# A planned RWKV-6 and feed-forward kernel: the planner's buffer rule, one chunk's banks, the fill products and the step order are changed

## The chip, the cores and the metric

The kernel runs on one core of a Trainium2 chip. A core has five engines, each with its own queue of instructions, worked in order: TensorE (PE) multiplies matrices into PSUM, VectorE (DVE) and ScalarE (ACT) do elementwise work, GpSimd (POOL) too, and SyncE (SP) issues transfers. The metric is the device time of one execution in microseconds (us), the median of several runs: before the change 566.9 us over 5 runs, from 564.67 to 569.37.

## The reference

First comes an RWKV-6 attention over 4 sequences, 8 heads, 768 tokens and 48 channels. Its output, 3072 tokens of 384 values, goes through a feed-forward layer of 2048 hidden values with a hard-swish. The weights of that layer come as float64, the rest as float32.

```python
state = np.zeros((B, H, D, D), dtype=np.float32)
for t in range(S):
    cur = np.einsum('bhd,bhe->bhde', u[None] * kt, vt)
    y[:, :, t] = np.einsum('bhd,bhde->bhe', rt, state + cur)
    state = wt[:, :, :, None] * state + np.einsum('bhd,bhe->bhde', kt, vt)
...
h = x @ w_in
relu6 = np.clip(h + 3.0, 0.0, 6.0)
g = h * relu6 / 6.0
return (g @ w_out).astype(np.float32)
```

## The kernel before

**Tiling.** The tokens are cut into 24 chunks of 128 (number i), and four chunks make a block (0 to 5). A chunk's attention is done for all heads at once, in two halves of 64 tokens. A block's 512 tokens then go through the feed-forward layer. Block 0 uses plain products, since its weights are still being loaded and converted from float64; blocks 1 to 5 use sums of weights and of operands, so that fewer products are needed. The feed-forward work of block b runs while the attention of block b+1 is made.

**Steps.** No instruction is written in its final place. Each piece of work is a named step, added to a planner (class Plan) with its engine, an assumed duration, the steps it comes after, a due time (key) and the buffers it holds until named steps have ended. Plan.order walks through an assumed time: of the engine that is free first it takes the open step with the lowest key that can start then. The instructions are emitted in that order, engine by engine, and the chip's queues keep it: a step that waits holds up all steps behind it on its engine.

The names that matter here, with i a chunk and b a block:

- SP: feat, tok, rkt (a chunk's inputs), fetch (weights), refetch (inputs read again for the vets), move, store.
- DVE: back and fore (scans of the decay), own (products for the diagonal), above (line 482, copies the masked scores out of two PSUM buffers, which gives them back), mid and state (the state), shift, join, full (float64 weights to float32), gate (hard-swish), sin and sout (sums of weights), tx (sums of operands), sum (sums of g), reads such as a3 or a10 (line 805), c12 and c22 (results), vet (checks the input range).
- ACT: diag (A's diagonal), turned (K out of PSUM), kvs, third and leave (y out of PSUM into x), low and whole (float64 weights), ramp and clip (hard-swish), s1, c11, c21.
- PE: dot, score, turn, kv; first and read (y of a chunk in block 0); begin and read (y of a later chunk; read also makes the next chunk's scores, in two buffers); up and down (feed-forward). up0.f.c is f of 16 products on chunks from c; upb.d.r is one of 20 products of half d; downb.p.k.x is part x of product k of pair p.
- POOL, from chunk 7 on: K, R, own, decay, decb.

**PSUM.** The tile "bank" is a ring of four PSUM buffers shared by score, up and down; "bankS" is one buffer; "y_ps" is a pair of banks for a chunk's y (and the next chunk's K-times-V in its free columns). The planner holds a count for each ring: a step that needs a buffer may start when enough of the held ones have ended, whichever these are. When the instructions are emitted, the tile pool gives out the real buffers by its own rule.

**Fill products.** Until the first up product, the emitter puts products without use (spin, line 1204) in front of PE steps that the plan starts late, one for each 0.22 us of three quarters of the gap. They write to "bank" buffers. One product of 512 columns (line 296) writes "bankS" at the start.

## Time and profile before

| what | value |
|---|---|
| runs, median (range) | 566.9 us (564.67 to 569.37) |
| profiled execution, its own time | 567.81 us |
| its span | 565.7 us |
| granted TensorE clock, mean | 0.99 |
| PE, DVE, ACT, POOL busy | 543.9, 453.1, 266.4, 105.2 us |
| moved by DMA | 63.96 MB, mean 113 GB/s |
| first up product starts | 31.81 us |
| first product of block 1, 2, 3, 4 starts | 151.25, 237.91, 323.44, 409.69 us |

The page gives each engine's busy time and its share of the span, then the span in 40 slices of 14 us with a digit for the busy tenths, and a row PEclk with the granted clock. A timeline row reads: start, duration, engine, line, operation, tile written and tiles read, shapes, number of records; in brackets, how long the engine was idle before it and what ended that. A product is two records. "Start to start" is the time from one step's first record to the next step's, which is what a step costs PE when nothing waits; a record's own duration is longer, since products overlap. PE's steps cost, start to start: up0 1.30 us, later up products 0.86, down products 1.30 (1.39 in block 0), read 1.52, begin 1.04. DVE's: join and full 0.88 and 0.87, gate 0.33 (block 0) and 0.60, sum of g 0.60, tx 1.71, 1.13, 0.79, 0.79, vet 1.66 for wflat or two times 0.86.

### The profile page before, as it was taken

What the parts mean: (1) busy time and instruction counts of PE and PEld (TensorE: products, weight loads), DVE (VectorE), ACT (ScalarE), POOL (GpSimd) and SP (SyncE); (2) the same over time, 40 slices, a digit from 0 to 9 for tenths busy, and PEclk for the clock granted to TensorE, in tenths of its full rate; (3) what the DMA queues carried; (4) which work ended last, traced back from release to release, by engine and by line L of the source; (5) the groups of instructions that cost most, each with busy time, mean ns of one, the idle gap of its engine ahead of it and who ended that gap; (6) DMA issues with size and microseconds to landing.
All of it is one profiled execution on the core that took longest, in us unless ns stands there. A gap on an engine that the chain in (4) does not pass through costs nothing.

```text
span 565.7 us, 13312 instructions
## 1 busy us (share of the span) xinstructions
PE 543.9 (96%) x5530; PEld 483.2 (85%) x5530; DVE 453.1 (80%) x727; ACT 266.4 (47%) x655; POOL 105.2 (19%) x111
## 2 busy tenths in 40 slices
PE   8999999999999999999998999998999999999995
PEld 7887787678887899888998988898988899988995
DVE  6989999999988977889997889997887836187440
ACT  3876784543365613556613555623465621255100
POOL 2000000126163114211334310425210100000000
PEclk9979999989999999999999999999999999999999
DMA  8949652631240365547423548333400001000001
GB/s 269 290 133 320 216 174 67 169 99 42 87 120 1 89 212 144 175 164 215 127 86 120 173 138 238 92 126 120 142 36 0 9 2 36 30 0 2 0 15 48
DMA packets 23077, 63.96 MB, mean 113 GB/s; under 512 B 3120, under 2 KB 10352, under 8 KB 23008
## 3 DMA queue, kind: packets, MB, share of 16 engines
q1 hardware_dynamic: 22880, 63.02, 35.9%
q8 instruction: 45, 0.74, 0.6%
q14 instruction: 24, 0.20, 0.1%
q10 hardware_dynamic: 128, 0.00, 0.0%
HBM read 57.31 MB, written 4.72 MB: 110 GB/s over the span
## 4 chain that ended last, share of the span: by engine, by line
PE 67%; DVE 24%; issue 3%; DMA 3%; ACT 2%; SPq 0%; DVEq 0%
PE bank L845 26%; PE bank L788 19%; PE bankS L845 5%; PE bank L674 4%; PE bankS L788 3%; DVE g L805 3%; DVE g L813 2%; PE y_ps L549 2%; DMA feat_in<-in_feat_dram 1%; DVE E L407 1%; DVE A L482 1%; PE ps L491 1%; PE y_ps L558 1%; DVE W L416 1%; DVE w_out L394 1%
## 5 line engine op out<-in xcount | busy, mean ns | idle before, releaser
L809 ACT ACTIVATE clip<-g,three 128x512 f32<-128x512 f32 x80 | 57.2, 720 | 55.9 <-DVE g L805 49.9
L805 DVE TENSOR_TENSOR g<-bank,g 128x512 f32<-128x512 f32 x80 | 54.2, 685 | 15.8 <-PE bank L788 15.3
L813 DVE SCALAR_TENSOR_TENSOR g<-clip,g 128x512 f32<-128x512 f32 x80 | 58.2, 737 | 10.7 <-ACT clip L809 10.7
L845 PE MATMUL bank<-w_out,g 128*128 128x192 f32 x352 | 62.6, 328 | 0.0
L845 PEld LDWEIGHTS bank<-w_out,g 128*128 128x128 f32 x352 | 57.9, 190 | 0.8
L427 POOL TENSOR_TENSOR K<-feat_in,E 112x512 f32<-112x512 f32 x17 | 22.1, 1299 | 150.1 <-DVE W L416 93.4
L466 ACT ACTIVATE A<-eyes,dg 128x64 f32<-128x64 f32 x192 | 48.9, 335 | 1.0 <-PE y_ps L558 0.5
L674 PE MATMUL bank<-xT,w_in 128*128 128x256 f32 x192 | 46.2, 393 | 0.0
L674 PEld LDWEIGHTS bank<-xT,w_in 128*128 128x128 f32 x192 | 36.9, 197 | 6.5 <-DVE A L482 0.5
L788 PE MATMUL bank<-xT,w_in 128*128 128x256 f32 x160 | 41.1, 381 | 1.1 <-DVE g L805 1.0
L641 ACT COPY xT<-y_ps 48x256 f32<-48x256 f32 x80 | 29.2, 365 | 25.8 <-PE y_ps L558 25.0
L861 ACT ACTIVATE o<-bank 128x192 f32<-128x192 f32 x33 | 10.9, 332 | 64.1 <-PE bank L845 64.1
L803 ACT COPY g<-bank 128x512 f32<-128x512 f32 x50 | 29.0, 580 | 19.6 <-PE bank L788 19.3
L788 PEld LDWEIGHTS bank<-xT,w_in 128*128 128x128 f32 x160 | 29.9, 190 | 5.6 <-DVE g L805 1.9
L431 POOL TENSOR_TENSOR W<-feat_in,W 112x512 f32<-112x512 f32 x17 | 21.7, 1274 | 62.9 <-DVE W L416 62.9
L407 DVE TENSOR_TENSOR_SCAN E<-feat_in,back 112x520 f32<-112x520 f32 x24 | 30.9, 1288 | 2.8 <-POOL K L427 1.6
L845 PE MATMUL bank<-more,g 128*128 128x192 f32 x176 | 30.7, 327 | 0.6 <-DVE o L863 0.6
L845 PE MATMUL bankS<-w_out,g 128*128 128x192 f32 x176 | 30.5, 327 | 0.8 <-ACT bankS L854 0.8
L788 PE MATMUL bank<-xT,bits 128*128 128x256 f32 x120 | 30.8, 379 | 0.0
L416 DVE TENSOR_TENSOR_SCAN W<-feat_in,start 112x520 f32<-112x520 f32 x24 | 29.5, 1230 | 0.3
L845 PEld LDWEIGHTS bankS<-w_out,g 128*128 128x128 f32 x176 | 28.8, 190 | 1.1 <-ACT bankS L854 1.1
L845 PEld LDWEIGHTS bank<-more,g 128*128 128x128 f32 x176 | 28.7, 190 | 1.0 <-DVE o L863 0.9
(278 smaller groups left out, 1163.0 us busy)
## 6 DMA issues: line engine op xcount, KB each, us to landing
feat_in<-in_feat_dram SPq DMA_DIRECT2D x23, 675.9 KB, 5.5
bits<-in_moe_w_in_dram SPq DMA_DIRECT2D x8, 768.0 KB, 9.6
bits<-in_moe_w_out_dram SPq DMA_DIRECT2D x8, 768.0 KB, 5.3
feat_in<-in_moe_w_in_dram SPq DMA_DIRECT2D x8, 768.0 KB, 4.6
feat_in<-in_moe_w_out_dram SPq DMA_DIRECT2D x8, 768.0 KB, 4.8
rk_in<-in_tok_dram SPq DMA_DIRECT2D x15, 384.0 KB, 5.6
v_in<-in_tok_dram SPq DMA_DIRECT2D x24, 192.0 KB, 3.7
out_dram<-o SPq DMA_DIRECT2D x24, 192.0 KB, 2.0
```

Of the source, the lines that this page charges most:

```text
L407: nc.vector.tensor_tensor_scan(out=E_[:, ::-1], data0=d["w"][:, :0:-1], data1=back.rearrange("q p t -> q (p t)")[:, ::-1], initial=0.0, op ...
L416: nc.vector.tensor_tensor_scan(out=W_, data0=d["w"][:, :-1], data1=starts[i % 2].rearrange("q p t -> q (p t)"), initial=0.0, op0=ALU.mult, ...
L427: early(i).tensor_mul(d["K"], d["k"], d["E"][:, :, 1:])
L466: nc.scalar.activation(out=d["A"][:, h, :], in_=eyes, func=ACT.Copy, scale=d["dg"][:, h])
L641: nc.scalar.copy(out=blocks[bk]["xT"][g * GP:g * GP + D, :, at:at + HL], in_=st[i]["y_ps"][(g ^ a) * GP:(g ^ a) * GP + D, a, :, :])
L674: nc.tensor.matmul(h_ps[:, :(c1 - c0) * L], lhsT=w_in[:, f // 2, j, f % 2, :], rhs=b["xT"][:, j, c0 * L:c1 * L], start=(j == 0), stop=(j = ...
L788: nc.tensor.matmul(b["p", d, c][:, z * HB:(z + 1) * HB], lhsT=weight(W_PLACE[r])[:, 2 * z + d, :], rhs=x_at(bk, X_PLACE[r]), start=fresh a ...
L803: nc.scalar.copy(out=out_, in_=src)
L805: nc.vector.tensor_tensor(out=out_, in0=src, in1=out_of(bk, d, other), op=ALU.add if sign > 0 else ALU.subtract)
L809: nc.scalar.activation(out=c, in_=out_of(bk, d, u), func=ACT.Relu, bias=three, scale=1.0)
L813: nc.vector.scalar_tensor_tensor(out=g, in0=blocks[bk]["r", d, u], scalar=6.0, in1=g, op0=ALU.min, op1=ALU.mult)
L845: nc.tensor.matmul(b["d", p, to][:, :h], lhsT=a, rhs=w(), start=(f == 0 and k in (1, 5)), stop=(f == HF - 1 and k in (2, 3, 4)), skip_grou ...
```

## The change

Five things change.

- The planner keeps a list of the buffers of each ring with the steps that free them. A step takes, of those whose freeing steps are already placed, the buffer whose last freeing step was placed first, and waits for that one buffer.
- Chunk 1's y no longer lies in "y_ps" but in two buffers of "bank"; third1 is four copies instead of two.
- The fill products write to a quarter of "bankS" in turn, only the first with start set; four of them stand at the start, in place of the 512-wide product. The emitter counts 0.28 us for one, and puts none before the first up product. There are 27 in the gaps instead of 39.
- Assumed durations and transfer sizes: those of first, third, read and leave of block 0 are larger, and those of the transfers change (a feature load counts 735 KB instead of 690, a fetch 546 instead of 768).
- The constants that set due times (LAG to TX) are new, and with them the order of steps on every engine. All steps and all instructions other than those above stay the same.

```diff
-LAG = 8.196
-AHEAD = -4.96
-LEAD = -2.25
+LAG = 11.816
+AHEAD = -12.641
+LEAD = 3.239
...
-START = (-127.21, -154.12, -36.12, -115.85, 30.64, 32.42)
-CONV = (-75.91, 4.42)
...
+APART = 1
+START = (-122.25, -133.43, -35.45, -193.52, 38.16, -10.0)
+CONV = (-81.21, 7.03)
...
-    SPIN = 0.22
+    SPIN = 0.28
...
+    def slot(self, r, slots, at, taken):
+
+        open_ = [(max((at[a] for a in frees or ()), default=-1), n) for n, frees in enumerate(slots[r])
+                 if (r, n) not in taken and all(a in at for a in frees or ())]
+        return min(open_)[1] if open_ else None
...
-                for n_, (r, _) in enumerate(hold):
-                    over = len(held[r]) + [x[0] for x in hold[:n_]].count(r) - self.rings[r]
-                    if over >= 0:
-                        ends = sorted(max(end[a] + (self.HOP[steps[a][0]] if steps[a][0] != engine else 0.0) for a in frees)
-                                      for frees in held[r] if all(a in end for a in frees))
-                        if len(ends) <= over:
-                            t = None
-                            break
-                        t = max(t, ends[over])
+                taken = []
+                for r, _ in hold:
+                    slot = self.slot(r, slots, at, taken)
+                    if slot is None:
+                        t = None
+                        break
+                    taken.append((r, slot))
+                    t = max([t] + [end[a] + (self.HOP[steps[a][0]] if steps[a][0] != engine else 0.0)
+                                   for a in slots[r][slot] or ()])
...
-            for r, frees in hold:
-                held[r].append(frees)
+            taken = []
+            for r, _ in hold:
+                taken.append((r, self.slot(r, slots, at, taken)))
+            for (r, slot), (_, frees) in zip(taken, hold):
+                slots[r][slot] = tuple(frees)
+            at[n] = len(out)
...
-                for _ in range(int(self.FILL * (self.start[n] - last) / self.SPIN)):
+                for _ in range(int(self.FILL * (self.start[n] - last) / self.SPIN) if n != self.until else 0):
...
-            nc.tensor.matmul(bank("bankS"), lhsT=ident[:PR], rhs=back.rearrange("q x t -> q (x t)")[:, :512], start=True, stop=True)
+            for _ in range(4):
+                spin()
...
         def new_y(i, alone=False):
+            started = set()
+            if i == APART and not alone:
+                st[i].update(started=started, y_ps=[bank()[:, :P * HL].rearrange("q (p t) -> q p t", p=P) for _ in range(2)])
+                return
...
+                if i == APART:
+                    for a in range(2):
+                        nc.scalar.copy(out=blocks[0]["x3"][rows, i * L + a * HL:i * L + (a + 1) * HL], in_=st[i]["y_ps"][a][rows, P - 1, :])
+                    continue
...
+            if i == APART:
+                y = [("bank", [f"leave{i}"])] * 2
...
-                plan.add(f"read{i}", "PE", 2.3 if first else 2.5, do(read_rest, i), [f"third{i}"] + [f"turned{i + 1}", f"tok{i + 1}"] * (i + 1 not in SOLO), t + 0.01)
+                plan.add(f"read{i}", "PE", (2.6 if first else 2.95) + 0.4 * (i + 1 not in SOLO), do(read_rest, i), [f"third{i}"] + [f"turned{i + 1}", f"tok{i + 1}"] * (i + 1 not in SOLO), t + 0.01)
...
+        still, spins = bank("bankS"), [-1]
+
         def spin():
-            nc.tensor.matmul(bank()[:, :L], lhsT=ident, rhs=ident, start=True, stop=True)
+
+            n_ = spins[0] = spins[0] + 1
+            at = n_ % 4 * L
+            nc.tensor.matmul(still[:, at:at + L], lhsT=ident, rhs=ident, start=n_ == 0, stop=True, skip_group_check=True)
```

On PE, the order around the start of a later block, before and after, for block 3 (the products of half 0):

```
before  down2.1.4.0 down2.1.4.1 read16 up3.0.1 up3.0.9 up3.0.14 up3.0.18 up3.0.3 up3.0.13
after   down2.1.4.0 down2.1.4.1 up3.0.1 read16 up3.0.3 up3.0.9 up3.0.18 up3.0.14 up3.0.13
```

and on DVE in the same place, and further back around the sums of g:

```
before  c22 state17 vet12 tx3.0 tx3.1 tx3.2 tx3.3 above17 fore18 vet13
after   c22 vet13 tx3.0 vet14 tx3.1 tx3.2 above17 tx3.3 fore18 vet15
before  sum2.0.2.1 mid15 sum17 back17 sum2.0.4.0 sum2.0.4.1 state15 fore16 c12 sum2.1.1 sum2.1.3 above15
after   fore16 sum2.0.2.1 state15 sum2.0.4.0 sum2.0.4.1 vet10 c12 sum2.1.1 sum2.1.3 above15
```

In the front, on PE: turn2 up0.12.0 score2 turn3 kv2 becomes turn2 up0.10.0 turn3 kv2 score2; dot8, which stood before up0.11.2, stands behind begin6, down0.1.1.0 and read6; begin7 moves behind down0.1.6.0; turn4 follows up0.5.2 in both. In block 1, down1.0.1.1 and down1.0.5.1 move behind down1.1.2.1, ahead of down1.0.2.0. K4 on DVE, which stood behind full12, stands behind full15 and one sum of weights.

## Prediction

> **What bounds the kernel now.** I read the page first (shares by engine, then the chain that ended last), then stretches of the span, then TensorE's timeline, and last what it waited for at the tile "bank".

> ```profile
> PE 543.9 (96%) x5530; PEld 483.2 (85%) x5530; DVE 453.1 (80%) x727; ACT 266.4 (47%) x655; POOL 105.2 (19%) x111
> ...
> PEclk9979999989999999999999999999999999999999
> ...
> PE 67%; DVE 24%; issue 3%; DMA 3%; ACT 2%; SPq 0%; DVEq 0%
> ```

> TensorE (PE) is 96% busy and carries 67% of the chain; VectorE (DVE) carries another 24%. All that an order of steps can win is TensorE's idle time, some 22 us (565.7 less 543.9), and what the clock takes: it falls in two slices (the 7 and the 8).

> ```profile
> 60.00:110.00 50.00, 49.67 (x657) 37.15 (x655) 48.27 (x78) 33.98 (x89) 2.40 (x2) 1.00 0.49 147
> ...
> 240.00:326.00 86.00, 83.28 (x896) 75.40 (x896) 77.25 (x119) 41.38 (x104) 24.31 (x24) 1.00 0.46 146
> ...
> 412.00:490.00 78.00, 77.19 (x660) 71.16 (x661) 48.20 (x91) 31.77 (x73) 3.90 (x5) 1.00 0.04 11
> ```

> Columns: stretch, length, busy time of PE, weight loads, DVE, ACT, POOL, granted clock. From 60 to 110 us PE and DVE are both full (49.67 and 48.27 of 50). From 240 on DVE has room (77.25 of 86), yet PE loses 2.7 us per block; from 412 on, where POOL is quiet, it loses next to nothing, and no step of mine touches that.

> ```profile
> its engine sat idle before it (us, times) until:
>   DVE A L482: 6.1, 6
> ```

> This is the tile "bank" (four buffers). Six times, 6.1 us in all, PE waited for the masked copy of the scores (step above), which gives two of the four back. In time order, with other waits of PE:

> ```profile
> 52.15 0.60 PE L491 MATMUL ps<-ident,K 112*128 112x112 f32 x4 [0.72 <-ACT kn L496]
> ...
> 58.40 0.27 PE L549 MATMUL y_ps<-W,S 48*48 48x64 f32 x2 [0.74 <-issue]
> ```

> ```profile
> 29.52 1.87 PE L450 MATMUL ps<-u_col,rk 112*128 112x2 f32 x8
> 31.24 0.78 PE L1204 MATMUL bank<-ident 128*128 128x128 f32 x2
> ```

> ```profile
> 111.41 1.02 PE L450 MATMUL ps<-u_col,rk 112*128 112x2 f32 x8 [1.28 <-DVE rk L440]
> 112.30 1.71 PE L674 MATMUL bank<-xT,w_in 128*128 128x256 f32 x6
> 113.80 4.31 PE L693 MATMUL bank<-w_out,g 128*128 128x384 f32 x8
> ...
> 133.45 0.67 PE L549 MATMUL y_ps<-W,S 48*48 48x64 f32 x32 [0.80 <-ACT kvs L578]
> ```

> ```profile
> 204.48 2.87 PE L845 MATMUL bankS<-w_out,g 128*128 128x192 f32 x16 [0.76 <-ACT bankS L854]
> ```

> ```profile
> 296.76 2.77 DVE L830 TENSOR_TENSOR S__3250<-g 128x512 f32<-128x512 f32 x2
> ...
> 297.65 1.33 POOL L444 TENSOR_TENSOR rk<-rk,u_bc 128x384 f32<-128x384 f32 x1
> ...
> 302.12 1.57 PE L845 MATMUL bank<-bits,S__3250 128*128 128x192 f32 x8 [1.42 <-DVE A L482]
> ```

> Seen here: at 31.24 a fill product stands between the last dot product and the first up product; at 111.41 PE waits 1.28 us and then runs slow for 3 us (4.31 us for eight records that take 2.85 elsewhere); at 296.76 two DVE sums take 2.77 us instead of two times 0.69 while POOL works, and PE pays at 302.12.

> **The change, part by part.** The step order comes from the two built programs; durations are start to start, from the profile before. The sum is made against the profiled execution: 567.81 us, 0.91 above the median of the runs (566.9).

> *Head.* Fill products fall from 39 to 27, plus 4 small ones for the 512-wide product at the start, and the one before up0.0.0 goes. They lie in PE's waits, so most cost nothing; their cover is the DVE chain through back1 and the masked copies. Fill 31.24 to 31.81 is not covered: the copy-out of chunk 1 (leave1) ended at 30.6. -0.57. Chunk 1's own banks lift first1's wait for leave0 (0.15 us), but the copy third1 becomes four instead of two (0.53 us now, some 0.9 by four copies of that half size), and leave1 still stands behind a 0.94 us weight copy (low3) that moved in front of it: 0.

> *Bank waits.* Waits 0.70 (240.61), 1.04 (326.48) and 0.90 (412.59) are product 14 of blocks 2, 3, 4, third in the order and in need of a bank. After, product 1 goes ahead of the read that takes two banks, and products 3 and 18, which need no fresh one, ahead of 14 (2.6 us or more from the read's end to 14, where it was 1.7); in blocks 2 and 3 the masked copy comes ahead of the last operand sum. Waits 1.42 (302.12) and 1.43 (388.38) are the C product of blocks 2 and 3, behind four DVE sums and above. The sums were slow because POOL's own18 and own22 ran beside them; after, fore16 and fore20 stand ahead of four DVE steps that wait for down products, so R16, decay16 and own18 (1.2 + 0.6 + 2.4 us) run within the 7.8 us of six down products, before the sums start. Without the stretch PE has 1.30 + 1.52 + 1.30 = 4.1 us, DVE needs 0.2 + 0.3 + 4 x 0.6 + 0.7 + 0.2 = 3.8. All five go: -5.49. (The sixth, 0.59 at 17.40, is a fill product's own.) What is late next: the first operand sum now stands behind one vet. PE has begin16 1.04 and two products, 3.64 us; DVE needs 0.2 + 0.27 + 1.72 (vet) + 1.71 (tx) + 0.2 = 4.1. A new wait of 0.46 in three blocks: +1.4.

> The rows show DVE adds stretched beside POOL (0.69 to 1.36). [...]

> *The dot product at 111.41.* dot8 waits for own8, late behind a stretched mid6 (1.16 us, usually 0.35). After, dot8 stands behind begin6, read6 and a down product. -1.34 for the wait, and with it the slow records behind it (4.31 less 2.85 = 1.46): -2.80.

> *Three single waits.* begin7 (0.80, kvs8 behind state7) moves behind down0.1.6.0 and state7 forward; s1 at 204.48 (0.76) gets two down products (2.6 us) as cover; up1.1.11 at 180.43 (1.00) waited for a read of DVE (a3) behind two sums of 1.37 each, one of which moves six steps back. -2.56.

> *Front, 35 to 100 us.* The waits 0.72 and 0.74 go: turn2 and turn3 are no longer both ahead of the copy between them, and first2 stands one product later. But K4 moves far back. Counting back to back from up0.0.0: PE reaches turn4 after 22 up products of 1.295, 2 x 2.53 reads, 4 x 1.39 downs and 7.0 of small steps = 46.1 us; DVE has from gate0.0.0, 2.85 us after up0.0.0 (behind R3, ending at 33.3, and shift3), 13 joins of 0.88, 13 fulls of 0.87, 12 shifts of 0.59, 19 gates of 0.33 and 8.9 of other steps = 45.0, plus 0.2. PE waits 1.95 there; 0.6 if the half clock lasts into the up products as before. I take 1.95, as DVE rows are stretched at times. Net +0.49.

> *SP and the vets.* Refetch and feature loads change places on SP; refetch0 now comes before feat13. Landing takes 4.3 to 4.8 us after the issue and the queue's packets fill 35.9% of the span; of 22 vets one waited before (2.6 us). Between nothing and 2.6 I take 0.

> *Waits no step of mine sees.* The whole order is new. Not fewer than none; not more than six of 1.0, the count and size that the bank had. I take two: +2.0, nearer the rows without a bank wait (three in 110 to 240 us).

> Sum: -0.57 - 5.49 + 1.4 - 2.80 - 2.56 + 0.49 + 2.0 = -7.53; 567.81 - 7.53 - 0.91 = 559.4 against the median.

> **Clock.** Granted clock is 0.50 from about 28.9 to 35.6 us though PE was busy 2.00 of 2.00 us from 26 to 28; there PE ran dot2 and read1, many small products. After 110 to 112 (busy 0.72 of 2.00) it is 0.50 again. I leave the first dip where it is: it costs the same in both. [...]

> **The rivals.**
> 1. *The front is held by DVE.* For: DVE 48.27 of 50 us. Then dot8 and begin7 (3.6 us) gain nothing: 559.4 + 3.6 = 563.0. Against: from 110 to 151 DVE is busy 39.3 of 41 us, so 1.7 are free.
> 2. *Half clock through the head.* For: fewer fills. first0, read0, first1 and read1 until 28.9 (0.67 + 2.97 + 0.67 + 2.4 = 6.7 us) would take twice as long: 566.1, no change. Against: the clock held through 16 to 18 us, PE busy 1.41 of 2.00.
> 3. *Vets stop DVE (slower).* Place: DVE's queue in blocks 1 to 3, where vet0, 1, 5 to 9 and 13 to 17 stand ahead of reads, sums or operand sums that PE needs. A vet whose words have not landed stops all behind it. Price up to a landing, 4.3 us, each. It decides when the twelve add over 10.3 us (569.7), 0.9 each; at 1.2 each it is 573.8. For: vet0 and vet1, at 194 and 202 us before, move into the first half of block 1, some 30 us forward. Against: one such wait in 22 before.
> 4. *The change does not do what it says* (buffers still not foreseen): five bank waits stay, 559.4 + 5.5 - 1.4 = 563.5.

> **How the numbers follow.** Forecast 0.50; rival 1 0.13; rival 2 0.11; rival 3 0.09; rival 4 0.09; a head without a dip and no unseen wait (559.4 - 2.0 - 2.4 = 555.0) 0.08. About 0.5% (2.8 us) is what measurement can tell. Faster by that means below 564.07: most of the forecast (0.48), of rivals 1 and 4 (0.16 of 0.22), 0.03 of rival 2, 0.08: 0.75. Slower, over 569.7: 0.09 and the ends of 1 and 2: 0.12. Same: 0.13. The likeliest case's own range is 555 to 563; with rivals 1, 2 and 4 and the better case, leaving out the slow rival and the ends, 552.5 to 567.5.

> **What would show it.** Right: the tile "bank" shows under 2 us of waits for above; the product at 31.24 is gone; eight down records at about 113 take 2.8 us again; own18 ends before the sums of block 2; a short wait at the first product of blocks 2 to 4. Wrong: DVE idle ahead of a vet; clock 0.50 before 25 us; turn4 waiting over 3 us; sums still at 1.36 with PE waiting behind.

## The result: a third of the gain that was forecast

The kernel after takes 564.4 us in the median of 52 runs (562.1 to 569.4); the kernel before took 566.9 beside it. The ratio is 0.9966, 95% interval 0.9955 to 0.9977: 1.3 to 2.6 us faster, inside the 0.5% that the prediction called "same". The forecast was 7.5 us. The profiled executions differ by 3.03 us (567.81 and 564.78; spans 565.7 and 562.7). A few slow runs, such as one of 639.4 us at a mean granted clock of 0.83, are left out of all comparisons.

The page of the kernel after: busy time, granted clock in 40 slices, shares of the chain.

```profile
PE 545.6 (97%) x5512; PEld 485.2 (86%) x5512; DVE 446.2 (79%) x727; ACT 266.6 (47%) x657; POOL 113.3 (20%) x111
...
PEclk9769989999999999999999999999999999999999
...
PE 68%; DVE 23%; DMA 3%; issue 2%; ACT 2%; SPq 1%; POOL 0%; DVEq 0%; POOLq 0%; ACTq 0%
```

PE's idle time (span less busy) fell from 21.8 to 17.1 us, 4.7. But its busy time grew by 1.7 us with less to do (fewer fill products). The clock digits point to the reason: 7, 6 and 8 in three slices of the first 84 us, where before had a 7 and an 8 in all. The bank waits, PE's waits at the tile "bank" in the kernel after:

```profile
its engine sat idle before it (us, times) until:
  DVE S__1392 L851: 1.3, 1
  DVE g L706: 1.0, 1
  DVE T__3500 L757: 0.9, 1
  DVE T__4359 L757: 0.9, 1
  DVE g L826: 0.8, 3
  DVE o L884: 0.5, 1
```

The line for the masked copy (6.1 us, six times) is gone, as forecast. In its place stand a sum of g (S__1392), a gate and the operand sums (T__). PE's rows of the kernel after in time order, at tiles of any name, with the idle time and what ended it in brackets:

```profile
11.39 1.05 PE L463 MATMUL ps<-u_col,rk 112*128 112x2 f32 x8 [0.72 <-ACT kn L509]
...
71.07 1.05 PE L463 MATMUL ps<-u_col,rk 112*128 112x2 f32 x8 [0.44 <-DVE rk L453]
71.98 2.79 PE L714 MATMUL bank<-w_out,g 128*128 128x384 f32 x4
...
130.51 1.35 PE L695 MATMUL bank<-xT,w_in 128*128 128x256 f32 x5 [1.03 <-DVE g L706]
...
145.30 1.57 PE L866 MATMUL bank<-w_out,S__1392 128*128 128x192 f32 x8 [1.27 <-DVE S__1392 L851]
```

The down product after dot4 (four records) takes 2.79 us, at a granted clock of 0.50 (72.11 to 75.53). So the dip that followed dot8's wait at 111 us before is gone, and there is one behind dot4 at 72.

Start times of the same steps give the account by segment:

| segment | forecast | profile |
|---|---|---|
| start to up0.2.0 (36.00, then 38.28) | -0.57 | +2.28 |
| to the first product of block 1 (151.25, 152.46) | -2.80 - 0.80 + 0.49 = -3.11 | -1.07 |
| to the last product of block 5 (558.39, 555.64) | -5.49 + 1.4 - 0.76 - 1.00 = -5.85 | -3.96 |
| unseen waits, end | +2.0 | -0.25 |
| sum | -7.53 | -3.0 |

### The profile page after: what moved, and what is told of

It is laid out like the page before. It is cut to its first block, busy times and chain, and to the rows that moved or that the text cites. A ratio compares the mean times of both kernels' runs of the same rounds, so it can differ in the third digit from the quotient of the medians.

```text
span 562.7 us, 13278 instructions
## 1 busy us (share of the span) xinstructions
PE 545.6 (97%) x5512; PEld 485.2 (86%) x5512; DVE 446.2 (79%) x727; ACT 266.6 (47%) x657; POOL 113.3 (20%) x111
## 4 chain that ended last, share of the span: by engine, by line
PE 68%; DVE 23%; DMA 3%; issue 2%; ACT 2%; SPq 1%; POOL 0%; DVEq 0%; POOLq 0%; ACTq 0%
PE bank L866 23%; PE bank L809 23%; PE bankS L866 5%; PE bank L695 4%; PE bankS L809 4%; DMA xT<-xT 2%; DVE g L826 2%; DVE W L429 2%; DVE E L420 2%; PE bank L488 1%; DVE g L834 1%; PE y_ps L566 1%; PE ps L504 1%; PE y_ps L588 1%; SPq L669 1%
## 5 line engine op out<-in xcount | busy, mean ns | idle before, releaser
L830 ACT ACTIVATE clip<-g,three 128x512 f32<-128x512 f32 x80 | 56.6, 719 | 44.2 <-DVE g L826 32.4
L440 POOL TENSOR_TENSOR K<-feat_in,E 112x512 f32<-112x512 f32 x17 | 23.0, 1350 | 153.2 <-DVE W L444 97.5
L695 PE MATMUL bank<-xT,w_in 128*128 128x256 f32 x192 | 47.9, 401 | 1.0 <-DVE g L706 1.0
L809 PE MATMUL bank<-xT,w_in 128*128 128x256 f32 x160 | 41.5, 382 | 0.0
L824 ACT COPY g<-bank 128x512 f32<-128x512 f32 x50 | 28.9, 580 | 17.2 <-PE bank L809 16.8
L444 POOL TENSOR_TENSOR W<-feat_in,W 112x512 f32<-112x512 f32 x17 | 22.0, 1295 | 67.2 <-DVE W L429 67.2
L809 PEld LDWEIGHTS bank<-xT,w_in 128*128 128x128 f32 x160 | 29.8, 190 | 4.9 <-DVE g L826 1.0
L429 DVE TENSOR_TENSOR_SCAN W<-feat_in,start 112x520 f32<-112x520 f32 x24 | 29.8, 1244 | 1.2 <-PE y_ps L566 0.7
```

The source lines that it names most:

```text
L429: nc.vector.tensor_tensor_scan(out=W_, data0=d["w"][:, :-1], data1=starts[i % 2].rearrange("q p t -> q (p t)"), initial=0.0, op0=ALU.mult, ...
L440: early(i).tensor_mul(d["K"], d["k"], d["E"][:, :, 1:])
L695: nc.tensor.matmul(h_ps[:, :(c1 - c0) * L], lhsT=w_in[:, f // 2, j, f % 2, :], rhs=b["xT"][:, j, c0 * L:c1 * L], start=(j == 0), stop=(j = ...
L809: nc.tensor.matmul(b["p", d, c][:, z * HB:(z + 1) * HB], lhsT=weight(W_PLACE[r])[:, 2 * z + d, :], rhs=x_at(bk, X_PLACE[r]), start=fresh a ...
L824: nc.scalar.copy(out=out_, in_=src)
L830: nc.scalar.activation(out=c, in_=out_of(bk, d, u), func=ACT.Relu, bias=three, scale=1.0)
```

## The experiments

Two readings stood against each other. Theory: too few fill products, so the head runs at half clock. Rivals: the new order alone makes the head late, or DVE holds the front whatever the head does. Later runs added the question of what the clock follows. "Lost clock" below is one minus the granted clock, times the span, as a mean over a kernel's runs: 5.4 us before (87 runs, clock 0.990), 10.7 after (54, 0.981).

### Fill products in the new order

```diff
-    SPIN = 0.28
+    SPIN = 0.22
```

> The kernel after, with 0.22 us counted for a fill product, as before the change, and nothing else: 38 fill products in the gaps instead of 27 (15 instead of 11 ahead of the first one, 5 instead of 3 or 4 in the later gaps); the order of steps is the same. Theory (the head ran at half clock because fills were taken out): the granted clock is 1.0 again from 14 to 21 us, up0.2.0 starts about 2.3 us earlier, near 36.0 instead of 38.3, and the time is 2 to 3 us less than after: about 562. Rival A (the new order, not the fills, makes the head late): no change of up0.2.0, 564.4. Rival B (the head is early, but DVE holds the front): up0.2.0 about 2 us earlier, but the first product of block 1 at 152.5 as after, 564.4.

Measured: 563.6 us, ratio 0.9956 (0.9933 to 0.9978); lost clock 7.1. Its mean is 1.3 us below that of after (standard errors 0.36 and 0.28). The theory's direction, half its size. In its profile the head still falls to half clock at 14.6 us, so the place was wrong; the later dip shrank from 10.2 to 3.4 us, and the one at 72 is missing. From 34 to 38 us, before, after and this run (granted clock third from the end):

```profile
34.00:36.00 2.00, 2.00 (x9) 1.69 (x8) 0.88 (x2) 1.27 (x2) 0.00 (x0) 0.74 0.00 0
36.00:38.00 2.00, 2.00 (x11) 1.77 (x10) 1.87 (x4) 1.71 (x4) 0.00 (x0) 1.00 0.00 0
```

```profile
34.00:36.00 2.00, 2.00 (x6) 1.56 (x5) 0.61 (x2) 1.70 (x8) 0.00 (x0) 0.50 0.00 0
36.00:38.00 2.00, 2.00 (x6) 1.64 (x5) 1.24 (x2) 1.21 (x2) 0.00 (x0) 0.51 0.00 0
```

```profile
34.00:36.00 2.00, 2.00 (x8) 1.63 (x7) 1.59 (x4) 1.22 (x4) 0.00 (x0) 0.74 0.00 0
36.00:38.00 2.00, 2.00 (x11) 1.76 (x10) 1.98 (x4) 1.88 (x4) 0.00 (x0) 1.00 0.00 0
```

The starting times in this profile decide between the sides: up0.2.0 starts at 36.29 (after: 38.28), which speaks against rival A, and the first product of block 1 at 149.91 (152.46), which speaks against rival B. A single profile could be chance, since the head's dip differs from execution to execution; but all five profiles of kernels with these 38 fills, this one and four below, have up0.2.0 between 36.05 and 37.01. Of the 2.55 us won up to block 1 here, 1.3 are left at the end: the waits at the first products of blocks 2 to 4 are 3.0 us instead of 2.2.

```diff
-    SPIN = 0.28
-    FILL = 0.75
+    SPIN = 0.20
+    FILL = 1.0
```

> The kernel after, with 0.20 us counted for a fill product and the whole of the gap filled instead of three quarters: 56 fill products instead of 27, same order of steps. Theory: the clock holds in the head until 26 us at least; 2 to 3.5 us less than after, 561 to 562. If fills begin to delay real products, the gain is smaller than with 38: 563. Rival A or B: 564.4 or more.

Measured: 565.6 us, 0.9971 (0.9949 to 0.9993); lost clock 6.4. The clock holds from the start to 29.8 us, yet first1 starts at 25.94, against 25.39 in after with half clock from 14 to 21. Up to first1 the head follows DVE (in after PE waits 0.45 us for DVE ahead of first1, in spite of the half clock); the half clock there cost nothing that shows, and with 56 fills first1 comes 0.55 us later. The dip comes at 29.8 us instead, three stretches long, and up0.2.0 starts at 39.25. A part of the theory falls: it is not the first dip that costs, but the one from 28 us on.

### Fill products in the old order

```diff
+        still, spins = bank("bankS"), [-1]
...
-            nc.tensor.matmul(bank()[:, :L], lhsT=ident, rhs=ident, start=True, stop=True)
+            n_ = spins[0] = spins[0] + 1
+            at = n_ % 4 * L
+            nc.tensor.matmul(still[:, at:at + L], lhsT=ident, rhs=ident, start=n_ == 0, stop=True, skip_group_check=True)
```

> The kernel before, with its 39 fill products in the same places but written to quarters of bankS instead of buffers of bank (four of them in place of the 512-wide product at the start). Order of steps and planner as before. It asks whether the place they write to matters by itself. Theory: the wait of 0.59 us at 17.40 (a fill product waiting for the masked copy) goes; 566.3 to 566.9, no difference. Rival: that wait and the one at 14.41 hold the head, and a head that flows gains 1 us or more: below 565.9.

Measured: 567.0, 0.9998 (0.9978 to 1.0019). Where fill products write makes no difference that could be measured. Next, this kernel with fewer of them:

```diff
-    SPIN = 0.22
+    SPIN = 0.28
...
-                for _ in range(int(self.FILL * (self.start[n] - last) / self.SPIN)):
+                for _ in range(int(self.FILL * (self.start[n] - last) / self.SPIN) if n != self.until else 0):
```

> The kernel before with the fill products of the change whole: written to bankS, 0.28 us counted for each, none ahead of the first up product: 29 in place of 39. Order of steps and planner as before. Theory: the granted clock falls to 0.5 early in the head, up0.2.0 starts some 2 us later than the 36.0 of before, and the time is about 2 us above that of the kernel with 39 of them: 568.5 to 569. Rival A (order, not fills): up0.2.0 at 36.0 or 0.5 earlier, 566.3 to 566.9.

Measured: 566.9, 1.0004 (0.9978 to 1.0029); lost clock 7.3 against 5.8. Ten fills fewer seem to cost clock, but 0.1 us of time (standard error 0.5). In its profile up0.2.0 starts at 35.38, where rival A had it, and not 2 us late. The theory's 2 us are not there in this order; so the missing gain is not a matter of the number of fills alone. Why the old order bears fewer fills stays open.

### What the clock follows

With 0.5-us windows one can read where the clock changes. In every trace, half clock lasts 3.41, 6.83, 10.24 us or more such steps, and within one execution the starts lie whole multiples of 3.4135 us apart (before: 28.20 and 113.54, 25.0 steps; after: 14.09, 27.74 and 72.11, 4.0 and 17.0 steps). Stretches of the kernel after on that grid:

```profile
17.50:20.91 3.41, 3.32 (x24) 2.74 (x24) 3.21 (x6) 2.70 (x6) 0.00 (x0) 0.50 1.02 219
20.91:24.33 3.42, 3.33 (x85) 3.06 (x84) 3.11 (x5) 1.85 (x4) 0.00 (x0) 1.00 1.05 207
24.33:27.74 3.41, 2.52 (x30) 2.07 (x28) 3.34 (x7) 1.94 (x10) 0.00 (x0) 1.00 1.04 333
27.74:31.15 3.41, 3.29 (x39) 2.97 (x42) 3.31 (x4) 2.93 (x10) 0.00 (x0) 0.50 0.92 336
31.15:34.57 3.42, 3.42 (x31) 3.10 (x24) 3.28 (x6) 2.04 (x9) 0.00 (x0) 0.50 0.13 44
34.57:37.98 3.41, 3.41 (x9) 2.69 (x9) 1.26 (x3) 2.33 (x7) 0.00 (x0) 0.50 0.00 0
...
68.70:72.11 3.41, 2.86 (x64) 2.50 (x64) 3.38 (x6) 2.56 (x5) 0.00 (x0) 1.00 1.02 310
72.11:75.53 3.42, 3.42 (x8) 2.03 (x8) 3.35 (x6) 2.56 (x6) 0.00 (x0) 0.50 0.71 266
```

The first number after the length is PE's busy time, the last but two the granted clock. From 31.15 PE is busy 3.42 of 3.42 us, and the next stretch has half clock; so there it isn't idleness of PE. What differs is what PE runs: dot products with 2 streamed columns, reads of y that use 48 rows and 48 columns. Take for each record rows x columns x streamed columns / (128 x 128), and add up the records that start in a stretch: up products at full clock give 4096 (after, 37.98 to 41.39), at half clock 2048 (34.57 to 37.98). Over the 638 stretches between 7 and 165 us of the 14 traces, each with its own grid:

| array use of a stretch | stretches | next one at half clock |
|---|---|---|
| under 1500 | 56 | 54 |
| 1500 to 1600 | 8 | 3 |
| over 1600 | 574 | 0 |

The two exceptions under 1500 stand at 1176 and 1412. The best bound on array use (1560) misses 3 of the 638 stretches. The same counting with the best bound on PE's busy time misses 53, on streamed columns 35.

Two runs test it, each with 11 more products, on 128 streamed columns, at the same places; in the second they use a sixteenth of the array.

```diff
+            for _ in range({2: 2, 4: 3}.get(i, 0)):
+                more()
...
+                if i == 2 and p % 2 or i == 3 and p == 1:
+                    more()
...
+        more = spin
```

> The kernel with 38 fills, and 11 more fill products of 128 x 128 on 128 columns among the small products: four around dot2, three in read1, one in dot3, three ahead of dot4. Theory (the granted clock of a stretch of 3.41 us follows how much of the array the stretch before it used, rows times columns times streamed columns; dot products and the reads of y use little of it though PE is never idle there): the half clock at 28 to 38 us and at 72 us goes or shrinks to one stretch of 3.4 us, the mean granted clock over the runs rises from 0.987 to 0.991 or more; the products themselves cost up to 11 x 0.215 = 2.4 us, the clock gives back 2 to 4: 562 to 564. Rival (only pauses of PE count, of which these fills remove hardly any): clock 0.987 or lower, and 565 to 566.

```diff
-        more = spin
+        def more():
+            nc.tensor.matmul(still[:32, :L], lhsT=ident[:32, :32], rhs=ident[:32], start=False, stop=True, skip_group_check=True)
```

> As the run with 11 more fill products, in the same places and with the same 128 columns, but on 32 rows and 32 columns of the array, a sixteenth of it. Theory: PE is as busy as in that run, but the array is not: the half clock at 28 to 38 us and at 72 us stays, mean granted clock 0.984 to 0.988, time 565 to 566.5. Rival (busy time or streamed columns count, not the part of the array): clock and time as with the large ones.

Measured: 565.2 us (0.9964, 0.9935 to 0.9993) with the large ones, 568.5 (1.0040, 1.0017 to 1.0063) with the small ones; lost clock 5.8 and 9.9. PE is as busy in both; from 60 to 80 us, first the large ones, then the small ones:

```profile
60.00:80.00 20.00, 19.56 (x216) 15.49 (x217) 19.32 (x30) 16.51 (x30) 0.00 (x0) 1.00 0.70 239
```

```profile
60.00:80.00 20.00, 19.56 (x204) 14.44 (x203) 19.13 (x30) 15.52 (x29) 0.00 (x0) 0.91 0.72 247
```

Busy 19.56 us in both, clock 1.00 and 0.91. So in this pair the clock goes with the part of the array in use, and not with busy time. On the grid of each run, the stretch at 71 or 72 us has PE busy 3.30 us in both; its array use is 1620 with the large ones, and full clock follows, and 898 with the small ones, and half clock follows. The pair also gives a price: 4.1 us of lost clock (9.9 less 5.8) come with 4.1 us of time (means 568.9 and 564.8, standard error of the difference 0.8). The numbers set for the large ones were missed, a clock of 0.990 instead of 0.991 and 565.2 instead of at most 564: in both profiles the head is at half clock for four stretches from 27 us on, and the 11 products were not paid back.

### The waits at the first products, and their cause

```diff
+    behind = (("up2.0.1", "read12"), ("up3.0.1", "read16"), ("up4.0.1", "read20"), ("refetch6", "move2.1.1"), ("refetch14", "move3.1.1"))
...
+        for n, to in self.behind:
+            order.remove(n)
+            order.insert(order.index(to) + 1, n)
```

> The kernel after with 0.22 us for a fill product (38 fills, the kernel of the first run), and five steps moved by hand: the first product of blocks 2, 3 and 4 stands behind the read again, as before the change, and the refetch that stood ahead of the moves of x on SP (blocks 2 and 3) stands behind them. Theory: the waits ahead of these first products (1.23, none seen and 1.75 us in that kernel; 0.43, 0.91, 0.86 in after) come from the transfer that moves half of x (issue 4.1 us, landing 3.1 us later), not from a vet; the read takes 1.52 us in the meantime, so they go, and no wait of PE over 0.3 us is left at these places: 561.5 us, 2 us less than the 563.6 of that kernel. Rival: the read now takes its two buffers first, product 18 or 14 waits for the masked copy again, 0.7 to 1.0 in three blocks: 563 to 564.

DVE's row for the first operand sum of block 3 in the kernel after, and SP's issues ahead of it:

```profile
318.60 0.43 DVE L757 SCALAR_TENSOR_TENSOR T__3500<-xT 128x256 f32<-128x256 f32 x1 [0.58 <-DMA xT<-xT]
```

```profile
310.88 0.33 SPq L906 DMA_DIRECT2D feat_in<-in_moe_w_out_dram  x1
311.26 4.11 SPq L669 DMA_DIRECT2D xT<-xT  x6
```

The sum waits for a transfer, behind a vet that had ended. Blocks 2 and 4 of the kernel after:

```profile
231.95 1.74 DVE L912 TENSOR_REDUCE w_max<-feat_in 128x1 f32<-128x1536 f32 x1
233.85 0.42 DVE L757 SCALAR_TENSOR_TENSOR T__2648<-xT 128x256 f32<-128x256 f32 x1 [0.15 <-DMA xT<-xT]
...
403.71 0.43 DVE L757 SCALAR_TENSOR_TENSOR T__4359<-xT 128x256 f32<-128x256 f32 x1 [0.54 <-DMA xT<-xT]
```

So in block 4 it is the transfer too; in block 2 a vet of 1.74 us ends 0.15 us before the transfer lands, and either would have held the sum. Measured with the read first: 563.0 us, 0.9944 (0.9920 to 0.9969). PE's rows at the same place:

```profile
318.66 1.13 PE L814 MATMUL bank<-T__3511,bits 128*128 128x256 f32 x4
320.46 1.13 PE L814 MATMUL bankS<-T__3511,w_in 128*128 128x256 f32 x4 [0.67 <-ACT bankS L822]
```

The waits at the first products are gone and no wait for the masked copy came back, but product 3, now directly behind product 1 (the read stood between them), waits 0.67 for ScalarE's copy of it, in two blocks. Of 2 us expected, 0.6 came. The run moved the reads and the refetches together; which of the two took the waits away was not taken apart.

### DVE at the end of the front

```diff
+            if n not in (13, 14, 15):
+                sum_of(weight(dst), weight(x), weight(y), sx, sy)
```

> The kernel with 38 fills, and the sums of weights 13, 14 and 15 left out (the output is then wrong; their three DVE instructions took 1.48, 1.37 and 1.66 us beside POOL in the profile of after). Theory (DVE holds the end of the front, as the first rival of the prediction had it): the waits of PE at 145 us (1.27) and 148.6 (0.46) go, the first product of block 1 comes 1.7 us earlier after up0.15.2 (20.2 us instead of 21.95), and the time is 1.7 us less: 561.9. Rival: another chain holds that stretch (above8, state8 and begin8): 0.4 us or less.

Measured: 562.9 us, 0.9929 (0.9904 to 0.9955). From up0.15.2 to the first product of block 1 it takes 20.41 us instead of 21.95: 1.54 of the 1.7 expected, and the wait of 1.27 is not there; the second one is (0.45). The time fell by 0.7 (means, standard error 0.6), with 0.4 us more lost clock: less than half of the 1.7, and no verdict by itself. By the length of the stretch DVE does hold it, as the first rival of the prediction said. DVE's rows of after there, and POOL's beside them:

```profile
138.22 1.37 DVE L851 TENSOR_TENSOR S__1392<-S__1392,g 128x512 f32<-128x512 f32 x1
139.51 1.48 DVE L761 TENSOR_TENSOR w_in<-w_in 128x512 f32<-128x512 f32 x1
141.03 1.37 DVE L759 TENSOR_TENSOR w_in<-bits,apart 128x512 f32<-128x512 f32 x1
142.32 1.66 DVE L757 SCALAR_TENSOR_TENSOR w_in<-w_in,T__1582 128x512 f32<-128x512 f32 x1
143.90 0.76 DVE L495 COPY_PREDICATED A<-mask,bank 128x256 f32<-128x256 uint8 x2
144.57 0.68 DVE L851 TENSOR_TENSOR S__1392<-g,S__1392 128x512 f32<-128x512 f32 x1
```

```profile
139.00 1.45 POOL L456 TENSOR_TENSOR rk<-rk_in 128x384 f32<-128x384 f32 x1
140.52 1.33 POOL L457 TENSOR_TENSOR rk<-rk,u_bc 128x384 f32<-128x384 f32 x1
141.81 1.62 POOL L440 TENSOR_TENSOR K<-feat_in,E 112x512 f32<-112x512 f32 x1
```

Adds that take 0.68 alone take 1.37 to 1.66 here, and the sum that PE waits for stands behind them. In blocks 2 and 3, where the prediction looked for slow sums with PE waiting behind (1.42 and 1.43 us before), the waits stayed away; slow adds with PE waiting behind came in the front instead (1.27 us).

### Which part of the change does it

The planner's rule alone, in the kernel before:

```diff
-                        t = max(t, ends[over])
...
+                    slot = self.slot(r, slots, at, taken)
...
+                    t = max([t] + [end[a] + (self.HOP[steps[a][0]] if steps[a][0] != engine else 0.0)
+                                   for a in slots[r][slot] or ()])
```

> The kernel before with the new buffer rule of the planner and nothing else. By the two programs it moves three steps of PE, all in block 2, and 17 of DVE; the reads stay ahead of product 14, and the four sums ahead of above15 and above19. Theory (the rule does nothing without the new due times): the bank waits at 240, 302, 326, 388 and 412 us (1.04 to 1.43 and 0.70 to 0.90) are there as before, and the time is 566.9, within 1 us. Rival (the rule foresees the waits and the planner avoids them): they go, 562 to 564.

Measured: 566.3, 0.9994 (0.9974 to 1.0013). PE's waits at "bank" are still there:

```profile
  DVE A L493: 5.1, 6
```

The rule alone changes nothing that could be measured (before: 6.1, 6). And with the old rule put back into the kernel after, the planner gives every engine the same steps in the same order; so the rule has no share in the gain. Next, the kernel after with the old due times, LAG to TX:

```diff
-LAG = 11.816
+LAG = 8.196
...
-START = (-122.25, -133.43, -35.45, -193.52, 38.16, -10.0)
+START = (-127.21, -154.12, -36.12, -115.85, 30.64, 32.42)
```

> The kernel after with the due times (LAG to TX) of before: the rule, chunk 1's banks, the fill products, and the new durations stay. 61 PE steps stand elsewhere than before the change. Theory (the gain lies in the new due times, the half clock in the 27 fill products): clock like that of the kernel before with few fills (0.987), one or two of the bank waits left, 565.5 to 567. Rival (durations and rule bring the gain): 563.5 or less.

Measured: 577.3 us (four runs), 1.0183 (1.0148 to 1.0218), some 10 us slower than before, which neither side expected. The page's clock row, and PE's waits at "bank" for the masked copy:

```profile
PEclk9559789999899999999999999999999999999998
...
  DVE A L495: 4.1, 4
```

Half clock lasts from 15 to 42 us, eight stretches in a row, and comes again at 66 (three) and 151; lost clock is 20 us on the mean. The waits for the masked copy are back with the old due times (4.1 us), so it was the new ones that took them away, with the new rule in both. Old due times don't go with the new durations; they can't be taken back alone, and the size of their share in the time stays open.

### A better version

Three steps more moved by hand in the kernel with the reads first, added to its list:

```diff
+    ("up2.0.3", "up2.0.9"), ("up3.0.3", "up3.0.9"), ("dot4", "down0.0.3")
```

> The kernel with 38 fills and the reads first, and three more steps moved by hand: product 3 of blocks 2 and 3 behind product 9 (PE waited 0.67 us in each for the copy of product 1), and dot4 behind the down product after it (it waited 0.33 for own4, and with read3 ahead of it made a stretch of 2.8 us that uses little of the array). Theory: those three waits go, 1.67 us, and the half clock at 65 to 76 us that came in some runs comes less often, 0.5 us on the mean: 561 us. Rival (waits move to the next product): 562.5 to 563, as without.

Measured: 562.5 us, 0.9933 (0.9908 to 0.9959), lost clock 6.2. The three waits are gone; others came (0.61 at product 11 of block 2, 0.48 at product 9 of block 4), and turn4 waits 1.03. Nearer the rival.

And four in the front:

```diff
+    ("sin14", "sum0.1.4.1"), ("sin15", "sin14"), ("down0.1.4.0", "begin8"), ("down0.1.4.1", "down0.1.4.0")
```

> As the kernel with three more steps moved, and four in the front: the sums of weights 14 and 15 on DVE behind the sum of g that down0.1.3.1 waits for (1.27 us), and begin8 ahead of the last two down products (0.47 us, where PE waits for the second result). No work is taken out. Theory (the order on DVE, not its load, makes these two waits): 1.3 to 1.7 us less than the kernel with three moved, 559.5. Rival (DVE is full there, as the run with three sums left out suggests): the first product of block 1 then waits for the operand sums instead, and less than 0.7 us is won.

Measured: 561.3 us, 0.9906 (0.9878 to 0.9933), 5.3 us below before: faster than both kernels, and 1.3 below the run without the four moves (1.8 by the means, standard error 0.7), the difference that the theory gave, though not its 559.5. From up0.15.2 to the first product of block 1 it takes 20.65 us instead of the 21.96 of the run without. PE's rows:

```profile
143.11 1.46 PE L872 MATMUL bank<-w_out,g 128*128 128x192 f32 x8
144.50 0.67 PE L572 MATMUL y_ps<-W,S 48*48 48x64 f32 x32
...
146.24 2.87 PE L872 MATMUL bank<-more,g 128*128 128x192 f32 x16 [0.54 <-DVE o L890]
149.10 1.10 PE L815 MATMUL bank<-T__1805,bits 128*128 128x256 f32 x4
```

The 1.27 us are gone, with no work taken out; the second wait stayed (0.54). So the order on DVE made that wait, and not its load alone.

## Why the prediction was wrong

The bank waits, the wait at dot8, the three single waits, the two waits of 0.72 and 0.74 in the front and the fill product before up0.0.0 went as forecast. The step that failed first is the one on the clock: the prediction held half clock in the head for the same before and after, and put no term on it. What failed, term by term:

- **Head, -0.57.** It measured +2.28 in the profile. The step that failed is the sentence "I leave the first dip where it is: it costs the same in both". The dip of before, read there as 28.9 to 35.6 us, lasts from 28.20 to 35.03, two stretches; in after it lasts three, 27.74 to 37.98. Lost clock doubled, from 5.4 to 10.7 us over the runs. Among the 54 runs of after, time and lost clock go together (correlation 0.90, 0.55 us of time for each us): 562.8 us where the clock was 0.986 or more (median of 17 runs), 567.2 at 0.9765 or less (15). At that slope the 5.3 us more are worth 2.9 us; by the two runs with 11 more products, 1.0 each, 5.3; by the first run, which lost 3.6 us less clock than after and 1.3 us of time, 0.36 each, 1.9. The second rival, half clock through the head, named the mechanism, but the dip it feared (up to 28 us) is free, and the one it took as constant costs.
- **The dot product, -2.80.** Right at 111 us. But dot4, which now waits 0.44 behind read3, makes such a stretch at 68.7 (array use 1182), and the half clock after it takes 1.67 us from two steps (2.59 instead of 1.39 and 1.77 instead of 1.30): the cost moved. In the prediction dot4 was no term at all.
- **Front, +0.49.** The wait of 1.95 at turn4 isn't in the profile, where PE came late; with the head 2 us earlier it is 0.95 (first run). In its place are 1.03 at up0.15.2 and 1.27 at down0.1.3.1. Rival 1 was put at 563.0 by not counting dot8 and begin7; it was right that DVE holds the front, and wrong about where.
- **New wait at the first products, 3 x 0.46 = +1.4.** 0.43, 0.91 and 0.86, 2.2 in sum. The size was near; the mechanism was wrong. The working had a vet on DVE and PE's time against DVE's, and gave SP's order nothing. In blocks 3 and 4 it is the transfer of x, whose six issues take 3.7 to 4.1 us on SP behind a refetch or a feature load; in block 2 the vet and the transfer end within 0.15 us of each other.
- **Bank waits, -5.49.** PE's waits over 0.3 us from block 1 on fell from 7.8 to 2.6 us. The segment won 3.96 only. Waits of any size fell by 4.6; the rest lies in the products themselves, which have other neighbours (in each of blocks 2 and 3 the score products in the reads take 0.3 more, the up products 0.2 to 0.3 more, the down products 0.2 less). No run takes that apart.
- **Unseen waits, +2.0.** 1.03, 1.27, 0.44 and 0.40 (a read in block 3), 3.1 in sum.
- **SP and the vets, 0.** Right as to the vets: none waits over 0.3 us for its words, and the third rival is out. The fourth rival (buffers not foreseen) is out too: the waits are gone, by the new due times and not by the rule.
- **Small slips in the working.** The row at 111.41 shows a wait of 1.28, where the sum takes 1.34; and no row or run gives the 2.4 us that the better case (555.0) takes off for a head without a dip.

What stays open is the exact share of the clock: between 1.9 and 5.3 of the 5.0 to 5.6 us that are missing, by which of the three prices is taken. The rest is waits and the products' own time.

## What to carry to other kernels

A wait that an order takes away is worth its full size only where the next resource has room: ask for each what stands next, on which queue. Count a half clock as a cost of its own: in these traces it followed 54 of the 56 stretches of 3.41 us with an array use under 1500 of 4096, whether PE was busy or not. So look for stretches in which TensorE runs small products, and try a large product that is needed anyway between them, or put waits elsewhere. Eleven large products without use lowered the lost clock (5.8 us against 7.1) and still cost time (565.2 us against 563.6). Compare mean granted clocks over many executions before a difference of 0.5% is read from two profiles.
